# A fused attention and two-layer MoE kernel: the first half of its operations in another order, and copies and subtractions on other engines

## The chip, the cores and the metric

The kernel runs on one core of a Trainium2 chip. A core has five engines that run side by side, each with its own instruction queue that it works off strictly in order: TensorE (PE, matrix multiplication), VectorE (DVE), ScalarE (ACT), GpSimd (POOL) and SyncE (SP, which here issues every DMA). They wait for each other by semaphores. The metric is the device time of one execution in microseconds; smaller is better.

## The reference, cut to what matters

```python
# attention: batch 4, heads 8, sequence S = 576, head size 64
scores = (q @ k.T) / sqrt(64)
cum    = cumsum(log(clip(f, 1e-4, 1)))                # a forget gate: 32 rows of 576
attn   = softmax(causal_mask(scores + cum[:, None] - cum[None, :]))
x      = (attn @ v) as (2304 tokens, 512)
# first layer, d_ff = 2048; w is delivered as float64
h = x @ w_in;  g = max(h, 0) + alpha * min(h, 0);  x = g @ w_out
# second layer, the same sizes
h = x @ w_in2; g = h * tanh(log1p(exp(h)));        out = g @ w_out2
```

## The kernel before

Nothing in this kernel is issued where it is written. The functions `stage_T`, `stage_M`, `stage_S`, `stage_R`, `stage_V`, `group_a` and `moe_block` only record operations in a `Plan`: 5,138 of them, each with a number, an engine, what it reads and writes, and a function that issues its instructions. At the end `emit` walks through one list of operation numbers and issues them. Since each engine works off its queue in order, this list sets the order on all five engines.

**Attention** runs over 16 pairs of heads. For each pair:
- `stage_T` copies q and k into the tiles `QM` and `KM` (ACT, L478). Three more rows of `KM` come by DMA (SP, L736) from the running sums of the forget gate; the running sums are made once, at the start, by a chain of DVE and ACT operations on the tile `Pt` (L689 to L695).
- `stage_M` finds each row's maximum: twelve matmuls (PE, L773) and after each a reduction on DVE (L780), which writes `nmx` or a column of `M`. They share three PSUM banks. Five transposes (PE, L792) and two copies turn `M` into the tile `BQ`.
- `stage_S` forms the scores in four pieces (PE, L817), ACT takes the exponential into `Pt` (L827), POOL masks the diagonal blocks (L835).
- `stage_R` adds five parts of `Pt` with four additions into `accp` (L853, of 896, 128, 640 and 384 columns; all on POOL before), and PE sums over partitions (L865).
- `stage_V` multiplies by v in two windows (PE, L899), and DVE writes the result to `X` (L905).

In pair 0 each matmul of `stage_M` and each piece of `stage_S` is followed by a dummy matmul (L676), and thirty such dummies, which need only the tile `ident` made by POOL, stand ahead of everything on PE.

The matmuls use PE's array in three shapes: 128 rows by 128 columns (L773, L792, and all of the MoE), 64 rows by 128 (L817), and 128 rows by 64 (L865, L899).

**The MoE** runs over six blocks of 384 tokens. Float64 weights come in by DMA and are put together as float32 by ACT and DVE (`wb`, L556 to L562), then split into a high and a low part, the low part by a subtraction (L488); activations are split in the same way (`xh`, `xl`, `g`). A product is three matmuls (L943 to L945, L1008 to L1010, L1019 to L1021). `group_a` computes the first four slices of the first layer for a block; for three blocks its matmuls are meant to fill gaps of the attention, between its matmuls on PE.

For a copy or a subtraction that can run on two or three engines, `add` picks its home. Before, this goes by the place of the operation in its stage: `ENG.get(key, ...)`, with 39 entries, so each repetition of a stage has the same home. The order before is a written list of the first 3,391 operations; the rest follow as the planner `schedule`, a list scheduler with priorities (`PRIO`) and assumed costs, puts them.

Of the kernel before, what the change touches and what calls it, by code (L numbers as in the profile page):

```python
# [174 lines left out]


class Plan:

    HOP = {"PE": 0.25, "ACT": 0.2, "DVE": 0.22, "POOL": 0.15, "SP": 1.0, "SWAP": 0.0}
    OWN = {"PE": 0.0, "ACT": 0.14, "DVE": 0.12, "POOL": 0.1, "SP": 1.0, "SWAP": 0.0}  # L190
# [1008 lines left out]
```

## Time and profile before

| what | value |
|---|---|
| median of 3 runs | 1011.56 us (1011.18 to 1013.09) |
| the profiled execution's own time | 1013.04 us |
| its span on the core | 1011.3 us |
| PE busy | 999.3 us (99%) |
| DVE, ACT, POOL busy | 740.1, 536.1, 341.8 us |

The profiled execution is one run at the upper edge of the three. The span is what its trace shows, from the first instruction to the last; 1.7 us of its time lie outside. A PE that is "busy" isn't a PE at full speed: matmuls are pipelined, and a matmul that waits inside the pipeline counts as busy.

### The profile page before, as it was taken

The page shows a single profiled execution, that of the slowest core. Times are in us where ns is not written, and L with a number is a line of the kernel's source. Part 1 is how long each engine was busy: PE and PEld are TensorE (multiplying, and loading weights), DVE is VectorE, ACT ScalarE, POOL GpSimd, SP SyncE. Part 2 cuts the span into 40 slices and gives each one's busy share as a digit, 9 for nine tenths or more (in the row PEclk, how much of TensorE's full clock was granted, in tenths as well). Part 3 has the DMA queues.
Part 4 walks back from the last instruction along what each step waited for, and adds up shares of the span by engine and source line. Part 5 has one row for each costly group of instructions (what it writes and reads, how often), then busy time and mean ns, then how long its engine had stood idle before and what let it go on. Part 6 is the DMA issues. An engine that isn't in the chain of part 4 may idle for free.

```text
span 1011.3 us, 16560 instructions
## 1 busy us (share of the span) xinstructions
PE 999.3 (99%) x5900; PEld 899.6 (89%) x5900; DVE 740.1 (73%) x1751; ACT 536.1 (53%) x1127; POOL 341.8 (34%) x351
## 2 busy tenths in 40 slices
PE   7999999999999999999999999999999999999998
PEld 6667777777999999999999999999998899989997
DVE  7787666555687765655666679877788888977975
ACT  5777676654555543233334466555454544555553
POOL 4676545545355421010101012342323322423321
PEclk9999999999999999999999999999999999999999
DMA  5344122120224323334443353000000000000000
GB/s 159 104 116 125 50 75 71 38 60 14 82 86 146 125 94 125 126 103 142 131 154 101 112 155 117 1 1 32 1 31 2 0 32 1 11 21 1 32 1 31
DMA packets 55394, 71.02 MB, mean 70 GB/s; under 512 B 6672, under 2 KB 32272, under 8 KB 55312
## 3 DMA queue, kind: packets, MB, share of 16 engines
q1 hardware_dynamic: 55312, 69.97, 21.9%
q8 instruction: 46, 0.75, 0.3%
q14 instruction: 36, 0.29, 0.1%
HBM read 56.60 MB, written 13.33 MB: 69 GB/s over the span
## 4 chain that ended last, share of the span: by engine, by line
PE 96%; DVE 3%; ACT 1%; issue 1%; DMA 0%; DVEq 0%; ACTq 0%
PE b L943 13%; PE b L945 13%; PE b L944 13%; PE b L1008 7%; PE b L1021 7%; PE b L1020 7%; PE b L1019 7%; PE b L1010 7%; PE b L1009 6%; PE b L817 6%; PE b L899 4%; PE b L773 3%; PE b L865 2%; PE b L792 1%; DVE junk L780 1%; DVE wb L558 1%
## 5 line engine op out<-in xcount | busy, mean ns | idle before, releaser
L943 PE MATMUL b<-xh,w 128*128 128x384 f32 x768 | 258.7, 337 | 0.2 <-DVE x L480 0.2
L945 PE MATMUL b<-xl,w 128*128 128x384 f32 x768 | 257.4, 335 | 0.0
L944 PE MATMUL b<-xh,w 128*128 128x384 f32 x768 | 257.2, 335 | 0.0
L1000 POOL TENSOR_TENSOR x<-x 128x384 f32<-128x384 f32 x96 | 112.3, 1171 | 250.3 <-DVE x L998 187.0
L943 PEld LDWEIGHTS b<-xh,w 128*128 128x128 f32 x768 | 144.2, 188 | 5.3 <-issue 1.0
L944 PEld LDWEIGHTS b<-xh,w 128*128 128x128 f32 x768 | 144.2, 188 | 3.1
L945 PEld LDWEIGHTS b<-xl,w 128*128 128x128 f32 x768 | 144.2, 188 | 0.0
L1008 PE MATMUL b<-g,w 128*128 128x384 f32 x384 | 130.1, 339 | 0.8 <-DVE x L971 0.7
L1010 PE MATMUL b<-g,w 128*128 128x384 f32 x384 | 128.4, 334 | 0.0
L1009 PE MATMUL b<-g,w 128*128 128x384 f32 x384 | 128.4, 334 | 0.0
L478 ACT CAST g<-x 128x384 fp32r<-128x384 f32 x120 | 61.4, 513 | 113.3 <-POOL x L1000 56.3
L1021 PE MATMUL b<-w,g 128*128 128x512 f32 x288 | 113.2, 393 | 0.0
L1020 PE MATMUL b<-w,g 128*128 128x512 f32 x288 | 113.0, 392 | 0.0
L1019 PE MATMUL b<-w,g 128*128 128x512 f32 x288 | 112.8, 392 | 0.0
L780 DVE CUSTOM_DVE_ANT_0 junk<-b,tri 128x320 f32<-128x320 f32 (+3 forms) x160 | 69.4, 434 | 45.9 <-PE b L773 36.1
L488 DVE TENSOR_TENSOR g<-x,g 128x384 fp32r<-128x384 f32 x102 | 73.3, 722 | 37.3 <-ACT g L478 36.7
L556 ACT ACTIVATE wb<-raw 128x256 f32<-128x256 f32 x128 | 52.9, 432 | 56.8 <-DMA raw<-in_moe_w_out_dram 27.6
L488 POOL TENSOR_TENSOR xl<-X,xh 128x384 fp32r<-128x384 f32 x18 | 20.8, 1161 | 168.6 <-ACT xh L478 165.8
L827 ACT ACTIVATE Pt<-b 128x288 f32<-128x288 f32 (+1 forms) x128 | 58.1, 502 | 33.4 <-PE b L817 31.4
L1008 PEld LDWEIGHTS b<-g,w 128*128 128x128 f32 x384 | 72.1, 188 | 3.6 <-DVE x L971 1.5
L558 DVE TENSOR_SCALAR wb<-wb 128x256 int32<-128x256 int32 x128 | 43.6, 356 | 42.6 <-ACT wb L556 42.2
L992 ACT ACTIVATE x<-x,two 128x384 f32<-128x384 f32 x96 | 58.6, 613 | 28.6 <-DVE x L990 28.3
(93 smaller groups left out, 1911.1 us busy)
## 6 DMA issues: line engine op xcount, KB each, us to landing
raw<-in_moe_w_in_dram SPq DMA_DIRECT2D x64, 256.0 KB
raw<-in_moe_w_out_dram SPq DMA_DIRECT2D x64, 256.0 KB
wd<-wb SPq DMA_DIRECT2D x32, 256.0 KB
raw<-wd SPq DMA_DIRECT2D x32, 256.0 KB
kt<-in_k_dram SPq DMA_DIRECT2D x16, 288.0 KB
qt<-in_q_dram SPq DMA_DIRECT2D x16, 288.0 KB
out_dram<-x SPq DMA_DIRECT2D x18, 256.0 KB
vt<-in_v_dram SPq DMA_DIRECT2D x16, 256.0 KB
```

The costliest lines, as they stand in the source:

```text
L488: plan.add(engs, 0.0, at, lambda e: (nc.gpsimd if e == "POOL" else nc.vector).tensor_tensor(out=out(), in0=in0(), in1=in1(), op=ALU.subtra ...
L780: nc.vector.tensor_tensor_reduce(out=junk[ql, :z - a], in0=ps()[ql, :z - a], in1=tri[ql, x0 + a:x0 + z], scale=-1.0, scalar=BIG if n == 0 ...
L943: nc.tensor.matmul(ps[:, :NB], w[:, 0, c], xh[c], start=(c == 0), stop=False)
L944: nc.tensor.matmul(ps[:, :NB], w[:, 1, c], xh[c], start=False, stop=False)
L945: nc.tensor.matmul(ps[:, :NB], w[:, 0, c], xl[c], start=False, stop=(c == KC - 1))
L1000: add("POOL", c_pool(NB, 2.2), lambda e, m: nc.gpsimd.tensor_tensor(out=m, in0=e, in1=m, op=ALU.mult), [ek, mk], [mk])
L1008: nc.tensor.matmul(ps[:, :NB], w[:, 0, c], g[:, 0], start=first, stop=False)
L1009: nc.tensor.matmul(ps[:, :NB], w[:, 1, c], g[:, 0], start=False, stop=False)
L1010: nc.tensor.matmul(ps[:, :NB], w[:, 0, c], g[:, 1], start=False, stop=last)
L1019: nc.tensor.matmul(ps, g[:, 0, sl], w[:, 0], start=first, stop=False)
L1020: nc.tensor.matmul(ps, g[:, 0, sl], w[:, 1], start=False, stop=False)
L1021: nc.tensor.matmul(ps, g[:, 1, sl], w[:, 0], start=False, stop=last)
```

## The change

The planner, `PRIO` and `ENG` go. All 5,138 operations stand in one written list, and the home of each copy and subtraction is looked up by the operation's own number, so that two repetitions of a stage can have different homes. The list differs from the order before in its first 2,600 places; the last 2,538 are the same. The same 5,138 operations are done, with the same numbers.

```diff
-PRIO = {'': {0: -17.5, 1: -17.2, ...
-ENG = {('A0g', 0): 'ACT', ('A0g', 2): 'ACT', ('A0g', 3): 'POOL', ...
 ORDER = [int(x) for x in """
-11 29 12 23 15 22 16 17 28 25 14 27 32 5 36 21 35 34 3 31 24 13 33 38 26 89 56 84 9 10 55 113 90 85 18 20 86
...
 """.split()]
+HOME = {}
+HOME.update(dict.fromkeys((int(x) for x in """
...
+""".split()), "ACT"))
...
     def add(self, eng, cost, at, fn, ...):
         n = len(self.ops)
-        key = tuple(self.key)
         self.key[1] += 1
-        at += PRIO.get(key[0], {}).get(key[1], 0.0)
         if isinstance(eng, dict):
-            alt, e = eng, ENG.get(key, next(iter(eng)))
-            eng, cost, f = e, alt[e], fn
+            e = HOME.get(n, next(iter(eng)))
+            eng, cost, f = e, eng[e], fn
             fn = lambda f=f: f(e)
...
-    def schedule(self, nexts, left, eng, cost, prio, lag, dma, uses=()):
...
     def emit(self):
+        done = [False] * len(self.ops)
+        left = [len(ns) for _, ns in self.uses]
...
+        spare = {g: list(range(len(x))) for g, x in self.groups.items()}
+        for n in ORDER:
+            assert all(done[d] for d in self.ops[n][4])
+            for u in mine[n]:
+                if ("use", u) not in self.taken:
+                    self.taken["use", u] = spare[self.uses[u][0]].pop(0)
+            self.ops[n][3]()
...
-        head = set(ORDER)
-        order = ORDER + [n for n in order if n not in head]
-        for n in order:
-            ops[n][3]()
```

Homes that change, counted over the whole program: 59 operations go from POOL to DVE (23 additions of `stage_R`, 21 subtractions of weights, 15 of activations), 34 from ACT to DVE (copies), 29 from DVE to POOL (subtractions of activations), 13 from DVE to ACT.

In the rows below, line numbers are those of each file: L780, L558, L560, L562 of before are L739, L517, L519, L521 of the changed file, L773 is L732, L865 is L824, L792 is L751, L899 is L858. `ISA` is the reduction and the short read of its result that follows it.

First DVE, from the running sum of the forget gate (L691 and L650) into the reductions of pair 0. Before:

```order
L691 SCALAR_TENSOR_TENSOR Pt_123<-Pt_123,tri 32x576
L697 MEMSET bvec 128x1
L697 MEMSET bvec 3x1 x2
L558 TENSOR_SCALAR wb_92<-wb_92 128x256 x2
L695 SCALAR_TENSOR_TENSOR Pt_123<-Pt_123 32x576
```

and, five rows and the first three reductions further on:

```order
L780 ISA M_142 128x1
L558 TENSOR_SCALAR wb_92<-wb_92 128x256
L780 ISA junk,M_142<-b_69,tri,nmx 128x256
L780 ISA M_142 128x1
L560 SCALAR_TENSOR_TENSOR wb_92<-raw_91,wb_92 128x256
L780 ISA junk,M_142<-b_70,tri 64x64
L780 ISA M_142 64x1
L562 SCALAR_TENSOR_TENSOR wb_92<-raw_91,wb_92 128x256
```

The changed kernel, from the same running sum on:

```order
L650 SCALAR_TENSOR_TENSOR Pt_123<-Pt_123,tri 32x576
L656 MEMSET bvec 128x1
L656 MEMSET bvec 3x1 x2
L654 SCALAR_TENSOR_TENSOR Pt_123<-Pt_123 32x576
L664 MEMSET KM_0_136 64x576
L517 TENSOR_SCALAR wb_92<-wb_92 128x256 x2
```

and from the end of its third reduction on:

```order
L739 ISA M_142 128x1
L739 ISA junk,M_142<-b_69,tri,nmx 128x256
L739 ISA M_142 128x1
L739 ISA junk,M_142<-b_70,tri 64x64
L739 ISA M_142 64x1
L739 ISA junk,M_142<-b_71,tri 64x64
L739 ISA M_142 64x1
```

The last operation of the gate's chain (L695, L654) now stands ahead of the weight operations, and between the reductions of pair 0 the weight operations stand later: six of them lie between the third and the tenth reduction before, one now. On the other engines at this place: on POOL `ident` is made first now, where five fills stood ahead of it; on SP the k of pair 0 is the second load, where it was the sixth, and the q of pair 2 and one load of `BK` stand ahead of the first weights of `w_out`; on ACT the two weight activations (L556) stand behind the first copy of k instead of ahead of it.

Then PE, where `stage_R` and `stage_V` of pair 0 stand between matmuls of pairs 1 and 2. Before:

```order
L773 MATMUL b_70<-KM_0_134,QM_0_130 128x192
L865 MATMUL b_65<-Pt_122,ones 64x128 x2
L865 MATMUL b_65<-accp,ones 64x160 x2
L865 MATMUL b_66<-accp,ones 64x288 x2
L773 MATMUL b_71<-KM_1_135,QM_1_131 128x192
L899 MATMUL b_69<-Pt_122,vt_145 64x256 x2
L899 MATMUL b_69<-Pt_122,vt_145 64x128 x2
L792 MATMUL b_67<-ident,M_142 128x128 x3
L792 MATMUL b_68<-ident,M_142 128x128 x2
L899 MATMUL b_70<-Pt_122,vt_145 64x320 x6
L899 MATMUL b_70<-Pt_122,vt_145 64x192 x2
L899 MATMUL b_70<-Pt_122,vt_145 64x64 x2
```

The changed kernel:

```order
L824 MATMUL b_68<-accp,ones 64x288 x2
L732 MATMUL b_69<-KM_0_136,QM_0_132 128x256
L732 MATMUL b_71<-KM_1_137,QM_1_133 128x320
L751 MATMUL b_65<-ident,M_142 128x128 x3
L751 MATMUL b_66<-ident,M_142 128x128 x2
L858 MATMUL b_70<-Pt_122,vt_145 64x320 x6
L858 MATMUL b_70<-Pt_122,vt_145 64x192 x2
L858 MATMUL b_70<-Pt_122,vt_145 64x64 x2
L858 MATMUL b_71<-Pt_122,vt_145 64x256 x2
L858 MATMUL b_71<-Pt_122,vt_145 64x128 x2
L776 MATMUL b_65<-qt_126,kt_129 128x448
```

The two windows of `stage_V`, which stood apart with matmuls of full shape ahead of and between them, follow each other now, and the next scores follow straight on them. Over the whole program the shape of the array changes from one matmul to the next 150 times before and 117 times now.

## Rows read from the trace of the kernel before

**Rows 1.** The page, part 1: busy us, share of the span, instructions.

```profile
PE 999.3 (99%) x5900; PEld 899.6 (89%) x5900; DVE 740.1 (73%) x1751; ACT 536.1 (53%) x1127; POOL 341.8 (34%) x351
```

**Rows 2.** Busy time by stretch: stretch, length, PE, PEld, DVE, ACT, POOL, clock, DMA.

```profile
0.00:25.00 25.00, 19.48 (x116) 16.50 (x116) 19.45 (x63) 13.47 (x25) 11.89 (x27) 0.91 0.51 161
...
450.00:500.00 50.00, 50.00 (x291) 50.00 (x290) 31.52 (x78) 17.93 (x43) 3.32 (x3) 1.00 0.42 132
...
sum 400.00, PE 397.21 PEld 337.75 DVE 276.77 ACT 236.43 POOL 186.08; mean PE 56.74 PEld 48.25 DVE 39.54 ACT 33.78 POOL 26.58
```

**Rows 3.** PE's longest wait: us in total, times, longest.

```profile
PE b L676 <- POOL ident masks.py:199: 3.8, 1, 3.8
```

**Rows 4.** Timelines of the first 21 us: start, length, engine, operation [idle before].

```profile
3.79 8.41 PE L676 MATMUL b<-ident 128*128 128x128 f32 x60 [3.79 <-POOL ident masks.py:199]
...
7.11 0.68 ACT L694 ACTIVATE Pt<-Pt 32x576 fp32r<-32x576 f32 x1 [0.41 <-DVE bvec L697]
...
7.33 1.65 DVE L558 TENSOR_SCALAR wb<-wb 128x256 int32<-128x256 int32 x2
8.89 0.74 DVE L695 SCALAR_TENSOR_TENSOR Pt<-Pt 32x576 fp32r<-32x576 f32 x1
...
9.71 1.57 SPq L736 DMA_DIRECT2D KM<-Pt  x2
...
12.39 0.49 DVE L780 CUSTOM_DVE_ANT_0 junk<-b,tri 128x320 f32<-128x320 f32 x1 [0.58 <-PE b L773]
...
13.72 0.48 DVE L780 CUSTOM_DVE_ANT_0 junk<-b,tri,nmx 128x256 f32<-128x256 f32 x1 [0.17 <-PE b L773]
...
14.70 0.29 DVE L558 TENSOR_SCALAR wb<-wb 128x256 int32<-128x256 int32 x1 [0.48 <-ACT wb L556]
14.90 0.48 DVE L780 CUSTOM_DVE_ANT_0 junk<-b,tri,nmx 128x256 f32<-128x256 f32 x1
...
20.66 0.36 DVE L780 CUSTOM_DVE_ANT_0 junk<-b,tri 128x192 f32<-128x192 f32 x1 [0.56 <-PE b L773]
```

**Rows 5.** The stretch of the slow clock, columns as in Rows 2.

```profile
20.50:27.30 6.80, 6.48 (x29) 4.38 (x27) 4.71 (x18) 3.58 (x8) 1.23 (x2) 0.50 0.25 85
```

**Rows 6.** The chain that ended last, 98 to 136 us: start, us, what.

```profile
99.81 0.80 PE b L899 x8
100.61 0.98 PE b L865 x12
101.59 2.05 PE b L899 x20
...
121.36 1.13 PE b L865 x12
...
128.85 2.21 PE b L899 x20
...
132.03 0.65 PE b L899 x8
```

**Rows 7.** Durations by shape and home: count, busy us, mean ns, idle before.

```profile
L853 POOL TENSOR_TENSOR accp<-Pt 128x896 f32<-128x896 f32 x16 | 33.7, 2106 | 3.2 <-PE b L865 1.8 <-ACT Pt L827 0.6 <-POOL Pt L835 0.6
...
L488 DVE TENSOR_TENSOR g<-X,g 128x384 fp32r<-128x384 f32 x72 | 41.2, 586 | 19.1 <-ACT g L478 18.9
...
L488 DVE TENSOR_TENSOR w<-raw,w 128x512 fp32r<-128x512 f32 x32 | 22.2, 713 | 7.1 <-ACT w L478 7.0
```

**Rows 8.** DVE from 20 to 140 us: busy time, and its longest wait.

```profile
20.00:140.00 120.00, 118.22 (x888) 86.05 (x888) 90.62 (x319) 88.21 (x182) 70.34 (x84) 0.97 0.32 94
...
DVE junk L780 <- PE b L773: 13.7, 18, 2.0
```

**Rows 9.** DVE and POOL from 33 to 37 us, and L558 over the whole run (min/median/max).

```profile
33.66 2.06 DVE L558 TENSOR_SCALAR wb<-wb 128x256 int32<-128x256 int32 x2
...
33.97 2.94 POOL L853 TENSOR_TENSOR accp<-accp,Pt 128x640 f32<-128x640 f32 x2
...
L558 DVE TENSOR_SCALAR wb<-wb x128: 277/285/1629, 7.3 to 568.1; 128x256 int32<-128x256 int32 x128
```

More of the change, by code (lines that the diff above doesn't have):

```diff
@@ L1 @@
 from contextlib import ExitStack
-from heapq import heappop, heappush
 import concourse.bass as bass
@@ L21 @@
-ENG = {('A0g', 0): 'ACT', ('A0g', 2): 'ACT', ('A0g', 3): 'POOL', ('A1g', 0): 'ACT', ('A2g', 2): 'ACT', ('A2g', 3): 'DVE', ('A3g', 0): 'DVE', ('AX', 1): 'DVE', ('AX', 2): 'ACT', ('AX', 3): 'DVE', ('AX', 4): 'ACT', ('AX', 5): 'DVE', ('AX', 7): 'DVE', ('B0', 4): 'DVE', ('B3', 4): 'DVE', ('H0', 4): 'ACT', ('H0', 7): 'DVE', ('H1', 13): 'ACT', ('H1', 14): 'DVE', ('NM2', 1): 'ACT', ('NM2', 2): 'ACT', ('O1', 3): 'DVE', ('O1', 5): 'ACT', ('R2', 3): 'POOL', ('T2', 2): 'ACT', ('T2', 3): 'ACT', ('WF', 2): 'DVE', ('X0', 0): 'ACT', ('X0', 1): 'POOL', ('X0', 2): 'ACT', ('X0', 3): 'POOL', ('X0', 4): 'ACT', ('X0', 6): 'ACT', ('X0', 7): 'POOL', ('X1', 0): 'ACT', ('X1', 3): 'POOL', ('X1', 5): 'POOL', ('X1', 6): 'ACT', ('X1', 7): 'POOL'}
@@ L25 @@
 ORDER = [int(x) for x in """
[150 rows of a table removed]
-""".split()]
-class Plan:
-    HOP = {"PE": 0.25, "ACT": 0.2, "DVE": 0.22, "POOL": 0.15, "SP": 1.0, "SWAP": 0.0}
-    OWN = {"PE": 0.0, "ACT": 0.14, "DVE": 0.12, "POOL": 0.1, "SP": 1.0, "SWAP": 0.0}
-    DMA_LAG = 0.65
-    PASSES = 10
-    SWITCH = 0.2
-    STAY = 1.5
[224 rows of a table added]
+""".split()]
+HOME = {}
+HOME.update(dict.fromkeys((int(x) for x in """
[4 rows of a table added]
+""".split()), "ACT"))
+HOME.update(dict.fromkeys((int(x) for x in """
[14 rows of a table added]
+""".split()), "DVE"))
+HOME.update(dict.fromkeys((int(x) for x in """
@@ L196, in __init__ @@
+2242 2244 2394 2396 2550 2552 2556 2706 2708 2712 3329 3331 3333 3616 3618 3620 3918 3920 3922 4220
+4222 4224 4522 4524 4526 4824 4826 4828
+""".split()), "POOL"))
+class Plan:
     def __init__(self):
@@ new lines, in emit @@
+    def emit(self):
+        done = [False] * len(self.ops)
+        left = [len(ns) for _, ns in self.uses]
+        mine = [[] for _ in self.ops]
+        for u, (_, ns) in enumerate(self.uses):
+            for n in ns:
+                mine[n].append(u)
+        spare = {g: list(range(len(x))) for g, x in self.groups.items()}
[5 more added lines that the diff above has]
+            self.ops[n][3]()
+            done[n] = True
+            for u in mine[n]:
@@ L320, in schedule @@
                 left[u] -= 1
                 if not left[u]:
-                    heappush(wait[eng[u]], (ready[u], prio[u], u))
-        return order, start, found
-    def emit(self):
-        ops = self.ops
-        N = range(len(ops))
-        eng = [o[0] for o in ops]
-        dma = [o[5] if o[0] == "SP" else 0.0 for o in ops]
-        def graph(found):
-            deps = [dict.fromkeys(o[4], True) for o in ops]
-            for u, (_, before) in found.items():
-                if before is not None:
-                    deps[self.uses[u][1][0]].update(dict.fromkeys(self.uses[before][1], True))
-            users = [[] for _ in ops]
-            for n in N:
-                for d in deps[n]:
-                    users[d].append(n)
-            return [list(d) for d in deps], users
-        def pace(slow):
-            cost = [o[1] * (1.0 if o[0] == "PE" else 1.0 + 0.1 * (slow - 1.0)) for o in ops]
-            return cost, {e: x * (slow if e != "SP" else (1.0 + slow) / 2) for e, x in self.HOP.items()}
-        def total(order, users, slow):
-            cost, hop = pace(slow)
-            ready, free, queue = [0.0] * len(ops), dict.fromkeys(eng, 0.0), 0.0
-            now, door = "", 0.0
-            for n in order:
-                e = eng[n]
-                start[n] = max(free[e], ready[n], door if ops[n][7] else 0.0)
-                end = start[n] + cost[n]
-                if ops[n][7]:
-                    door = end
-                if e == "PE":
-                    end += self.SWITCH if ops[n][6] != now else 0.0
-                    now = ops[n][6]
-                free[e] = end
-                if dma[n]:
-                    end = queue = max(queue, end + self.DMA_LAG) + dma[n]
-                for u in users[n]:
-                    ready[u] = max(ready[u], end + (hop[e] if eng[u] != e else self.OWN[e]))
-            return max(free.values())
-        cost, hop = pace(1.2)
-        start = [0.0] * len(ops)
-        prio = [o[2] for o in ops]
-        best = None
-        deps0, users0 = graph({})
-        for _ in range(self.PASSES):
-            order, at, found = self.schedule(
-                users0, [len(d) for d in deps0], eng, cost, prio,
-                lambda a, b: hop[eng[a]] if eng[b] != eng[a] else self.OWN[eng[a]], dma, self.uses)
-            deps, users = graph(found)
-            t = sum(total(order, users, x) for x in (1.0, 1.2, 1.6))
-            if best is None or t < best[0]:
-                best = (t, order, found, users)
-            _, back, _ = self.schedule(
-                deps, [len(u) for u in users], eng, cost, [-at[n] - cost[n] for n in N],
-                lambda a, b: (hop[eng[b]] if eng[a] != eng[b] else self.OWN[eng[b]]) + dma[b] + self.DMA_LAG * (dma[b] > 0), None)
-            prio = [-back[n] - cost[n] for n in N]
-        _, order, found, users = best
-        head = set(ORDER)
-        order = ORDER + [n for n in order if n not in head]
-        self.taken = {("use", u): b for u, (b, _) in found.items()}
-        for n in order:
-            ops[n][3]()
-        self.start = start
-        self.total = total(order, users, 1.0)
@@ L394, in fox_attention__then__moe_prelu__then__moe_mish @@
+                    spare[self.uses[u][0]].append(self.taken["use", u])
+        assert all(done)
 @with_exitstack
```

65 lines of the change are left out of this document (removed), and 391 rows, old and new, of tables (HOME, ORDER).

## The prediction

> **What bounds the kernel now.** I read the page first: PE is busy for 999.3 us, 99% of the span [rows 1]. So only PE's own time counts, and the first question is where PE isn't dense. The table of busy time by stretch says it [rows 2]: 5.5 us of idle PE in the first 25 us, 2.8 us in the 400 us behind that (400 less 397.2), and none from 450 to 500 us, inside the MoE. The changed half of the order covers the attention and a part of the first MoE layer. In the MoE part PE has nothing to win; whatever the change brings must come from the attention, roughly the first 300 us, and whatever it brings there shifts everything behind it, since a full PE follows.
>
> The list of waits names one long one, 3.8 us for `ident` at the very start [rows 3]. That is little of the loss that a gapless PE could win. The larger part of PE's loss stands in no list of waits, because a matmul that is held up inside the pipeline counts as busy. Two things of that kind are visible: a price for each change of the array's shape, and a stretch of half clock early on. Both come below.
>
> **The change part by part.**
>
> *The start.* The timelines of the first 21 us [rows 4] show the chain on which the first reductions hang: ACT's scaling of the running sum (L694) ends at 7.79 us; DVE's last operation of the gate (L695) could begin there plus a hop, at about 8.0, but stands behind two weight operations and begins at 8.89; SP issues the rows of `KM` at 9.71, as soon as it ends; the first reduction begins at 12.39. In the new order L695 comes first: 0.9 us earlier. Between reductions, DVE then sits 0.48 us waiting for an ACT weight operation at 14.70, with the fourth reduction queued behind it: that one starts at 14.90, 1.18 us after the third (13.72), where the first three came 0.67 apart (12.39 to 13.72). The new order has no weight work there, which gives back 0.5 us, and five more weight operations leave the stretch, of which I count 0.2 us, since they fitted mostly beside the reductions' waits. Sum: 1.6 us by the twelfth reduction (20.66), on which transposes and first scores hang. Bounds: 0.7, if the copies of q and k on ACT hold up the start (two weight operations now stand among them), and 2.9, if all five others count at 0.29 us like the one at 14.70. The earlier `ident` lets the thirty dummies begin earlier, by up to the 3.79 us that they wait now. It is worth nothing: they take 8.4 us and then end before the rows of `KM` can land, and PE has a hole of up to 2.9 us (3.8 less 0.9) ahead of the first maximum. On SP the loads for pairs 0 and 2 move ahead of the first weights of `w_out`; only `group_a` needs those, later on PE: nothing.
>
> *Half clock.* From 20.5 to 27.3 us the granted clock is 0.50, the lower level, 1.2 GHz, with PE busy 6.48 of 6.80 us [rows 5]. From 450 to 500 us it is 1.00, 2.4 GHz [rows 2]. What PE did before it fell: the dummies until 12 us, and then matmuls paced by the reductions, one in some 0.7 us. The new order keeps this shape, a little denser. So I leave the stretch as it is: 0. Bounds: one half of 6.8 us, 3.4 us, won if it goes, or lost if the new hole brings another one.
>
> *Changes of shape.* The chain of work shows the price of one [rows 6]. The same eight, twelve and twenty matmuls appear with and without one: L899 x8 takes 0.80 us behind matmuls of full shape and 0.65 inside a run of its own shape; L865 x12 1.13 and 0.98; L899 x20 2.21 and 2.05. That is 0.15 us per change. The new order has 117 instead of 150, 33 fewer, nearly all behind pair 1: 33 x 0.15 is 5.0 us. Some of them stood where PE waited for an operand anyway; I take 0.13 each, 4.2 us. Bounds: 3.3 (0.10 each) and 5.3 (0.16).
>
> *PE's other waits.* The 2.8 us of visible idle behind 25 us [rows 2] are waits for reductions, exponentials and copies. A new order can take them away or make others. I take half as won, 1.4 us; bounds 0 and 2.8.
>
> *Other homes.* Ten of the 23 additions that move from POOL to DVE belong to pairs 0 to 7. The trace has no such addition on DVE. Its POOL price for 896 columns is 2106 ns; the nearest rows on DVE are subtractions of two SBUF operands, 586 ns for 384 columns and 713 for 512 [rows 7], about 1 ns a column, so 896 columns are 1.09 us, 640 are 0.84, 384 are 0.59, 128 are 0.33. Three, one, four and two of these are 7.1 us more on DVE; four subtractions of activations go the other way there, 2.3 us less. Net 4.8 us more in a stretch where DVE is busy 90.6 of 120 us and itself waits 13.7 us for the very matmuls PE is late with [rows 8]. So most of it lies beside DVE's waits: I count a quarter, 1.2 us of loss. Bounds 0 and 4.8. Behind 300 us the moves add work to DVE, with PE at full and DVE busy 31.5 of 50 us [rows 2]: nothing, as long as no product comes late.
>
> *Sum.* 1.6 + 4.2 + 1.4 - 1.2 = 6.0 us. Against the profiled execution's 1013.04 us that is 1007.0; this run was 1.5 us above the median, so against the median of 1011.56 it is 1005.6 us.
>
> **A rule that bears on the homes.** In the trace, two DVE operations (L558) take 2.06 us together at 33.66, while POOL works on two additions; over the whole run this operation has a median of 285 ns and a maximum of 1629 [rows 9]. So DVE and POOL seem to hold each other up. The Trainium skill says in "SBUF — State Buffer", "Who interferes with whom", that a DVE instruction with two SBUF inputs contends with a GpSimd instruction that reads SBUF. By that rule each addition moved to DVE could wait for whatever POOL is doing. It speaks against the move, and makes a rival below.
>
> **The rivals.**
>
> *A larger gain*, 1000 us: the half clock goes, or the waits hidden inside "busy" go as well. For it: PE's early matmuls come denser, without weight work between the reductions. Worked out: 6.0 + 3.4 for the clock and 1.4 for the other half of the visible waits is 10.8, 1000.8 us. Against it: the reductions still pace PE until about 20 us, and PE gets a hole at 10 us.
>
> *No change*, 1011 us: a merged run of one shape has to wait for the last of its operands, so that each change saved becomes a wait of the same size. For it: both windows of `stage_V` now follow each other and need `uu` of the same pair. Then 4.2 us turn to nothing, and so do the 1.4 of the waits; 1.6 - 1.2 are left, 1011.2. Against it: between them PE has work of other pairs and of `group_a` in the order.
>
> *DVE and POOL hold each other up*, on the other side. The place is the attention, where 23 additions and eight subtractions move to DVE while POOL still runs masks and the other additions. The price by the trace: L558's largest excess was 1.3 us (1629 less 285 ns); I take 0.5, between nothing and that, and 31 x 0.5 is some 16 us of DVE time. It decides against the gain when more than 7.2 of these 16 us come to lie on PE's path, since 6.0 + 1.2 are won otherwise. With 10 of them, 1011.56 - 7.2 + 10 is 1014.4 us. Against it: each of these operations leaves POOL, so there is less to meet; POOL was busy 70.3 of 120 us [rows 8].
>
> *Another stretch of half clock* costs 3.4 us and still ends at 1009.0; it is inside the forecast's own range.
>
> **How the numbers follow.** A measurement of this kernel can't tell differences under about 0.2%, 2.0 us, from none. Chances: the forecast, from 1001.5 to 1009.5 us, 0.56; the larger gain 0.20; no change 0.13; DVE and POOL 0.11. Faster is the first two, 0.76; same 0.13; slower 0.11. The predicted time is 1005.6 us. The range reaches from the larger gain, 1000.0, to 1011.6: it leaves out the slower case and the third of the larger gain that may lie below 1000, 0.18 in all.
>
> **What would show it.** Right: the first reduction at about 11.5 us and the twelfth near 19; L865 x12 mostly at 0.98; no weight operation of more than 0.5 us ahead of a reduction; PE as dense as before behind 300 us, and the whole MoE shifted by some 6 us. Wrong: additions L853 on DVE well above 1.1 us for 896 columns, PE waiting for them (behind `accp`) or for `X`; a second stretch at clock 0.50; waits of PE in the first MoE layer, on `w` or `g`, where there were none.

## The result and the profile after

| what | before | changed |
|---|---|---|
| median | 1011.82 us, 7 runs (1011.18 to 1017.25) | 1020.44 us, 7 runs (1019.39 to 1023.66) |
| ratio to before, 95% interval | | 1.0087 [1.0064, 1.0110] |
| profiled execution, its span | 1013.04, 1011.3 us | 1020.44, 1018.7 us |

The change makes the kernel slower, by 8.8 us going by the ratio (8.6 by the medians). The forecast was 1005.6 us and faster; the time lies outside its range, on the other side. The first part of the changed kernel's page answers to [rows 1]: PE has the same number of instructions and is busy for the same time, in a longer span, so what was added is waiting.

```profile
PE 998.4 (98%) x5900; PEld 902.2 (89%) x5900; DVE 778.8 (76%) x1802; ACT 525.2 (52%) x1106; POOL 294.0 (29%) x321
```

**Where the time goes.** The table of busy time by stretch of the changed kernel answers to [rows 2] (stretch, length, PE, PEld, DVE, ACT, POOL, clock, DMA share, GB/s):

```profile
0.00:25.00 25.00, 19.67 (x112) 17.28 (x113) 18.28 (x57) 13.13 (x23) 10.21 (x27) 0.91 0.47 150
...
50.00:75.00 25.00, 23.23 (x186) 15.92 (x185) 20.97 (x72) 17.42 (x37) 16.31 (x21) 1.00 0.34 93
...
300.00:350.00 50.00, 48.85 (x278) 47.60 (x277) 45.85 (x106) 26.88 (x63) 10.80 (x8) 1.00 0.34 111
350.00:400.00 50.00, 49.50 (x284) 48.98 (x283) 36.49 (x84) 17.26 (x39) 7.61 (x7) 1.00 0.36 116
400.00:450.00 50.00, 46.84 (x268) 45.88 (x267) 30.85 (x66) 12.39 (x30) 8.14 (x7) 1.00 0.32 97
450.00:500.00 50.00, 48.55 (x277) 47.56 (x276) 31.62 (x77) 16.40 (x41) 3.30 (x3) 1.00 0.41 129
```

From 300 to 500 us, where PE had been dense, it is now idle for 6.3 us. Waits inside the pipeline come on top. To see them I asked of both traces when PE had done equal amounts of its work (each matmul group counted with its undisturbed time). The changed kernel against the profiled execution of before, in us; the places are an estimate, since other choices of the undisturbed time move them by tens of us of work, while the loss from the lowest point on stays at 9.7 to 9.9 us:

```
PE work done      20    50   120   180   220   260   300   340   380   400   440   460 to the end
changed - before +1.2  +2.3  +0.4  -0.8  -2.4  -2.5  -0.7  +0.8  +2.3  +4.8  +7.0  +7.4
```

So the start loses, the attention behind 50 us gains some 4 to 5, and between 260 and 460 us of work, the first MoE layer, 9.9 us are lost; nothing happens behind it. The list of PE's waits from 310 to 500 us (total, times, longest) names what [rows 2] had none of:

```profile
PE b L902 <- DVE X L927: 2.7, 4, 1.3
PE b L902 <- DVE X L930: 2.5, 2, 2.3
PE b L968 <- DVE w L447: 0.5, 1, 0.5
```

L927 and L930 (before: L968, L971) are, in `prelu`, the activation of the first layer, the DVE operations that read a slice's PSUM bank last: L927 where the first operation of `prelu` was on ACT (L921), L930 where it was on DVE (L923). The first matmul L902 (before: L943) of a slice waits for one of them because only it frees the bank that the slice four further on uses. How much room there is can be read from both traces, from 310 to 500 us: from the end of that operation to the L902 that takes the bank, before, a median of 3.8 us over 47 slices, and under 0.5 us once; after, 1.5 us over 44, and under 0.5 us twelve times.

The chain of work of the changed kernel around its longest wait (start, us, what) shows who is late:

```profile
422.36 0.42 DVE wb L521
422.78 0.48 DVE g L447
423.26 0.14 SPq L550
...
423.91 4.67 DMA raw<-in_moe_w_in_dram
...
428.69 0.43 ACT wb L515
429.12 0.39 ACT X L921
...
429.53 0.04 DVE X L927
...
430.06 0.61 DVE X L923
...
431.06 0.56 DVE X L930
...
431.66 0.44 PE b L902
```

Read it upwards. The L902 at 431.66 waits for L930, which with its L923 finishes the slice that held the bank; the product of that slice was there at 426.8 us. Both stand in DVE's queue behind L927 of another slice, and that waits for its L921 on ACT. The product of this L921 was there at 422.1 us, and the part of `X` that it writes was free when POOL had read it, at 425.7:

```profile
424.70 1.01 POOL L447 TENSOR_TENSOR g<-X,g 128x384 fp32r<-128x384 f32 x1 [3.67 <-ACT g L437]
```

But ahead of it in ACT's queue stands L515, a conversion of a weight for the second layer (not needed before 570 us) whose load lands at 428.6. The load was issued late, since DVE freed its buffer late. So an operation that could have run waits 3.3 us behind one that can't, and a second queue waits behind it.

**The start.** The timeline of the first 21 us answers to [rows 4]:

```profile
3.82 1.43 DVE L648 TENSOR_SCALAR Pt<-Pt 32x576 f32<-32x576 f32 x1
...
6.71 1.34 DVE L650 TENSOR_TENSOR_SCAN Pt<-Pt,tri 32x576 f32<-32x576 f32 x1
...
8.80 0.75 DVE L654 SCALAR_TENSOR_TENSOR Pt<-Pt 32x576 fp32r<-32x576 f32 x1 [0.52 <-ACT Pt L653]
...
12.30 0.48 DVE L739 CUSTOM_DVE_ANT_0 junk<-b,tri 128x320 f32<-128x320 f32 x1
...
12.44 0.41 SPq L683 DMA_DIRECT2D qt<-in_q_dram  x1
...
16.58 1.36 ACT L437 CAST QM<-qt 64x576 fp32r<-64x576 f32 x2 [3.30 <-DMA qt<-in_q_dram]
...
17.20 0.49 DVE L739 CUSTOM_DVE_ANT_0 junk<-b,tri 128x320 f32<-128x320 f32 x1
...
19.28 0.29 DVE L517 TENSOR_SCALAR wb<-wb 128x256 int32<-128x256 int32 x1 [1.58 <-ACT wb L515]
19.48 0.48 DVE L739 CUSTOM_DVE_ANT_0 junk<-b,tri 128x320 f32<-128x320 f32 x1
...
20.74 0.35 DVE L739 CUSTOM_DVE_ANT_0 junk<-b,tri 128x192 f32<-128x192 f32 x1
...
20.90 0.61 PE L732 MATMUL b<-KM,QM 128*128 128x320 f32 x1 [2.54 <-DVE wb L519]
```

L654 is 0.1 us earlier, not 0.9; the twelfth reduction comes at 20.74, before at 20.66. The ninth reduction, at 17.20, is early, but the tenth stands behind a conversion, which waits for ACT, which waits for a load of q: the same pattern as at 428 us. The stretch of lower clock of [rows 5] has become longer, 10.0 us instead of 6.8:

```profile
20.50:27.30 6.80, 6.40 (x24) 5.06 (x26) 4.69 (x21) 4.88 (x10) 1.67 (x2) 0.50 0.40 121
27.30:30.50 3.20, 3.20 (x16) 2.22 (x14) 1.29 (x6) 0.88 (x2) 0.00 (x0) 0.50 0.00 0
```

### The profile page after: what moved, and what is told of

Read it like the earlier page. It is cut to its first block, busy times and chain, and to the rows that moved or that the text cites. A ratio compares the mean times of both kernels' runs of the same rounds, so it can differ in the third digit from the quotient of the medians.

```text
span 1018.7 us, 16555 instructions
## 1 busy us (share of the span) xinstructions
PE 998.4 (98%) x5900; PEld 902.2 (89%) x5900; DVE 778.8 (76%) x1802; ACT 525.2 (52%) x1106; POOL 294.0 (29%) x321
## 4 chain that ended last, share of the span: by engine, by line
PE 80%; DVE 9%; DMA 5%; issue 2%; ACT 2%; SPq 1%; DVEq 0%; ACTq 0%
PE b L902 11%; PE b L904 11%; PE b L903 11%; PE b L980 7%; PE b L979 7%; PE b L978 7%; PE b L776 5%; PE b L967 4%; PE b L968 4%; PE b L969 4%; PE b L858 4%; PE b L732 3%; DMA raw<-in_moe_w_out_dram 2%; DVE wb L521 2%; DVE wb L519 2%
## 5 line engine op out<-in xcount | busy, mean ns | idle before, releaser
L902 PE MATMUL b<-xh,w 128*128 128x384 f32 x768 | 259.2, 338 | 5.3 <-DVE X L927 2.7
L902 PEld LDWEIGHTS b<-xh,w 128*128 128x128 f32 x768 | 144.2, 188 | 12.0 <-DVE X L927 4.7
L968 PE MATMUL b<-g,w 128*128 128x384 f32 x384 | 128.6, 335 | 0.5 <-DVE w L447 0.5
L739 DVE CUSTOM_DVE_ANT_0 junk<-b,tri 128x320 f32<-128x320 f32 (+3 forms) x160 | 69.4, 434 | 34.0 <-PE b L732 25.4
L515 ACT ACTIVATE wb<-raw 128x256 f32<-128x256 f32 x128 | 52.5, 431 | 81.3 <-DMA raw<-in_moe_w_out_dram 29.5
L517 DVE TENSOR_SCALAR wb<-wb 128x256 int32<-128x256 int32 x128 | 41.9, 336 | 51.9 <-ACT wb L515 51.2
L786 ACT ACTIVATE Pt<-b 128x288 f32<-128x288 f32 (+1 forms) x128 | 57.7, 503 | 36.7 <-PE b L776 30.5
L969 PEld LDWEIGHTS b<-g,w 128*128 128x128 f32 x384 | 72.1, 188 | 2.3 <-DVE g L447 2.3
L967 PEld LDWEIGHTS b<-g,w 128*128 128x128 f32 x384 | 72.1, 188 | 1.5 <-issue 1.1
```

What stands on the lines that cost most here:

```text
L739: nc.vector.tensor_tensor_reduce(out=junk[ql, :z - a], in0=ps()[ql, :z - a], in1=tri[ql, x0 + a:x0 + z], scale=-1.0, scalar=BIG if n == 0 ...
L902: nc.tensor.matmul(ps[:, :NB], w[:, 0, c], xh[c], start=(c == 0), stop=False)
L967: nc.tensor.matmul(ps[:, :NB], w[:, 0, c], g[:, 0], start=first, stop=False)
L968: nc.tensor.matmul(ps[:, :NB], w[:, 1, c], g[:, 0], start=False, stop=False)
L969: nc.tensor.matmul(ps[:, :NB], w[:, 0, c], g[:, 1], start=False, stop=last)
```

## The experiments

Each kernel carries a written list and homes of its own; "hybrid" is the new attention with the old first layer. Ratios are to the kernel before, run on the same chip in the same batch.

**Which part, and order or homes.** Two kernels take the change apart by kind, two by place (the cut is the last matmul group L858 of the attention, at some 255 us).

```diff
 # e1_order: new ORDER, old HOME        # e2_homes: old ORDER, new HOME
 # e3_att:
-ORDER = new
+head = new[:new.index(last_L858) + 1]
+ORDER = head + [n for n in old if n not in head]
+HOME = new homes for head, old homes behind
 # e4_moe: the same with old and new exchanged
```

> The new order with the old homes. Theory 'order': in the first MoE layer the new order puts weight conversions that wait for their DMA ahead of the activation operations on ACT and DVE, so PE waits for its PSUM banks there whatever the homes are; then the loss stays and the time is 1018 to 1022 us. Theory 'homes': DVE, busy 90 of 100 us from 250 to 350 us because of the operations moved to it, is late by itself; then the loss of some 10 us goes and the time is 1008 to 1012 us. Theory 'pair': the order was fitted to its homes, and each alone is worse than both together: over 1023 us.

Measured: 1051.16 us, 1.0382 [1.0365, 1.0400].

> The old order with the new homes. Theory 'order': about the time of before, 1010 to 1014 us. Theory 'homes': DVE gets the added work in the old order as well, and the time is 1018 to 1022 us. Theory 'pair': slower than the changed kernel, over 1023 us, since subtractions now run on engines whose queues were ordered for other work.

Measured: 1033.30 us, 1.0224 [1.0203, 1.0245].

> New order and homes up to the last attention matmul of L858 (some 255 us), behind it the old order and the old homes. Both theories put the loss behind this point: the time is that of before less the 2.5 us that the attention gained in the trace, 1008 to 1010 us, and PE is dense from 260 us on. If the loss is a debt of the attention (weights or slices left over that the first MoE layer has to make up for), it stays: 1014 to 1020 us.

Measured: 1010.43 us, 0.9985 [0.9975, 0.9995]. The time lies just above the range expected; PE is dense from 300 us on.

> Old order and homes up to the last attention matmul of L858, new ones behind it. Both theories: before's time plus the loss of the first MoE layer, some 10 us: 1020 to 1024 us. If the loss is a debt of the new attention: 1010 to 1014 us.

Measured: 1023.80 us, 1.0114 [1.0098, 1.0130].

The places are clear: the attention gains 1.5 us and the first layer loses 11.5 behind the old attention, 10.3 behind the new one (1.0087 against 0.9985). The kinds are not: order and homes hold only together, as the third theory said. A fifth kernel asked the same of the first layer alone:

```diff
-HOME = new homes
+HOME = new homes up to the last L858, old homes behind; ORDER = new
```

> The changed kernel with the old homes behind the last attention matmul of L858 only; order unchanged. Theory 'waiting conversions': the loss stays, 1018 to 1022 us. Theory 'DVE too full': the loss goes, 1009 to 1012 us. Theory 'pair' (the order holds only with the durations it was made with; POOL takes 1.2 us where DVE takes 0.6): slower than the changed kernel, over 1023 us, most of it here, since the whole order with old homes lost 13 us of PE time between 250 and 350 us.

Measured: 1035.37 us, 1.0217 [1.0201, 1.0233]. "DVE too full" was expected to gain here and lost 13 us (1.0217 against 1.0087). This says that POOL's and ACT's longer times don't fit the new order, not that DVE is innocent.

**Operations behind waiting conversions.** In the changed kernel's list only the places of second-layer conversions against other operations of ACT and DVE were changed, for example around 428 us on ACT:

```diff
 L437 CAST g<-X 128x384
-L515 ACTIVATE wb<-raw 128x256
 L921 ACTIVATE X<-b 128x384
+L515 ACTIVATE wb<-raw 128x256
 L515 ACTIVATE wb<-raw 128x256
```

> The changed kernel, with one thing moved: from 380 to 505 us, activation operations that by its trace were ready earlier go ahead of the conversions of second-layer weights on ACT and DVE that stood before them and waited for their load; 22 operations on ACT go ahead so, the order on PE is the same. Theory 'waiting conversions' (the loss comes from operations queued on ACT and DVE behind conversions whose load hasn't landed): the waits of PE at 405, 418, 429, 484 and 490 us go (0.5, 0.7, 2.4, 0.4 and 1.6 us, 5.6 in all), 1013 to 1016 us. Theory 'DVE too full' (the loss comes from the operations that moved to DVE): no change, 1018 to 1022 us.

Measured: 1016.84 us, 1.0042 [1.0023, 1.0061], a gain as 'waiting conversions' says, but short of its range.

> The kernel with activation operations put ahead of waiting conversions, once more: in its own trace one wait of 1.9 us for a DVE operation behind conversions is left at 486 us, with a stretch of lower clock behind it; 25 more operations on ACT and DVE go ahead of conversions of second-layer weights between 350 and 505 us. Theory 'waiting conversions': that wait and the low clock behind it go, and the slow half of its runs with them: 1012 to 1015 us. Rival: moving them only moves the wait on, 1016 to 1019 us.

Measured: 1014.14 us, 1.0027 [1.0014, 1.0039]. The wait at 486 us is gone, as expected; runs of up to 1017.7 us are not. The busy time of this second kernel, against the last two rows of the changed one above:

```profile
400.00:450.00 50.00, 50.00 (x289) 49.74 (x288) 31.98 (x72) 15.49 (x37) 7.95 (x7) 1.00 0.32 100
450.00:500.00 50.00, 50.00 (x291) 49.95 (x290) 33.69 (x85) 16.48 (x42) 4.34 (x4) 1.00 0.41 127
```

The 4.6 us of idle PE from 400 to 500 us are gone with DVE as busy as before, and with the same homes. Of the 8.8 us, 6.1 came back (1.0087 against 1.0027; by the two intervals together, between 3.5 and 8.7) by order on ACT and DVE alone: the queues of PE, POOL and SP are those of the changed kernel. That is the main cause, shown.

Two kernels put all weight work behind the cut, loads and stores too, at the other kernel's places, counted in matmul groups of PE:

```diff
-weight work (load_w, store_w) at the new places      # f2: at the old places
+weight work at the old places, in the new order      # f2: at the new places, in the old order
```

> The changed kernel with the weight work behind the last L858 (loads, conversions, splits, stores) at the places, and with the homes, that it had before, counted in matmul groups of PE; everything else as changed. Theory 'waiting conversions': the conversions come where their loads have landed, 1010 to 1014 us. Theory 'DVE too full': the other moved operations stay, 1017 to 1021 us. If the old places only fit the old order of the activations, more waits appear: over 1022 us.

Measured: 1074.86 us, 1.0610 [1.0590, 1.0629].

> The kernel before with only the weight work behind the last L858 at its new places and homes. Theory 'waiting conversions': the loss appears here, 1017 to 1022 us. Theory 'DVE too full': a third of the added DVE work comes along (19 subtractions of 0.7 us), 1011 to 1014 us.

Measured: 1088.08 us, 1.0737 [1.0720, 1.0755]. The first falls under its third case (over 1022 us), the second is far outside of both theories; the places fit only the list that they come from. They tell nothing between the theories.

**What is left in the first layer.** The second kernel still loses some 4 us of PE between 260 and 370 us.

```diff
-L515, L517, L519, L521, L437, L447 of first-layer weights, 255 to 380 us, ahead of activations that are ready earlier
+the same behind them
```

> The kernel with activation operations ahead of waiting conversions of second-layer weights, and now also ahead of the weight work of the first layer from 255 to 380 us (67 operations on ACT and DVE go ahead). In its parent's trace PE still loses some 4 us there: 1.25 at 267, 0.7 at 311, 1.1 at 328, 0.3 at 348, 0.6 at 370. Theory 'waiting conversions': they go, 1009.5 to 1012 us. Rival 'DVE too full' (there the work itself is late: operations of DVE take two to three times as long beside POOL's subtractions, and DVE is 90% busy): the weights come late in place of the activations, 1013 to 1018 us.

Measured: 1025.52 us, 1.0125 [1.0102, 1.0149], slower than either theory said. Now the weights come late; PE's waits from 255 to 380 us begin with

```profile
PE b L902 <- ACT x L437: 1.7, 2, 1.2
PE b L967 <- ACT w L437: 1.6, 1, 1.6
```

Here both kinds of work are needed at once, and putting all of one ahead cost more than it gave. So this cure does not reach the rest; whether a choice between single operations would, no run shows. Taking work off DVE there:

```diff
-HOME: seven first operations of the activation on DVE, two subtractions of X on DVE (299 to 370 us)
+HOME: seven on ACT, two on POOL
```

> The kernel with activation operations ahead of waiting conversions of second-layer weights, with nine of DVE's added operations between 299 and 370 us back at their old homes: seven first operations of the activation to ACT, two subtractions to POOL; same order. 5.4 us less on DVE, where it is 90% busy. If the loss that is left (4 us between 260 and 370 us) comes from a DVE that is too full there: 1 to 2 us faster than its parent, 1011.5 to 1013 us. Theory 'pair' (any home other than the one the order was made with makes something late): slower, 1015 to 1020 us.

Measured: 1014.27 us, 1.0018 [1.0001, 1.0036]. It can't be told from its parent, and lies between the two expectations. The two subtractions on POOL add to what DVE meets there: PE's waits for the subtraction of `g` from 255 to 380 us are 3.0 us, 1.8 in the parent. So this run doesn't rule out a DVE that is too full, which in the parent is busy for 4.00 of 4 us from 264 to 268 us and for 3.93 from 326 to 330, where PE loses. A place in the parent's timeline shows one thing that a schedule of fixed durations can't know:

```profile
327.48 1.29 POOL L447 TENSOR_TENSOR w<-wb,w 128x512 fp32r<-128x512 f32 x1 [4.98 <-ACT w L437]
327.99 1.19 DVE L447 TENSOR_TENSOR g<-X,g 128x384 fp32r<-128x384 f32 x1
...
329.24 0.44 PE L969 MATMUL b<-g,w 128*128 128x384 f32 x1 [0.81 <-DVE g L447]
```

The subtraction of `g` takes 1.19 us beside POOL where its median is 0.55, and PE waits for it. How much of the 4 us comes from this was not tried by itself.

**The start.** From the hybrid, first the conversions between the ninth and the twelfth reduction were moved, then one load as well.

```diff
 # h1_front, DVE
-L517 TENSOR_SCALAR wb_92<-wb_92 128x256
 L739 ISA junk,M_142<-b_71,tri 128x320
...
 L739 ISA M_142 128x1
-L519 SCALAR_TENSOR_TENSOR wb_92<-raw_91,wb_92 128x256
+L517 TENSOR_SCALAR wb_92<-wb_92 128x256 x2
+L519 SCALAR_TENSOR_TENSOR wb_92<-raw_91,wb_92 128x256 x2
 # t1_load, SP
 L683 DMA kt_128<-in_k_dram 128x576
+L683 DMA qt_125<-in_q_dram 128x576
 L695 DMA KM_0_134<-Pt_123 3x1x576
...
-L683 DMA qt_125<-in_q_dram 128x576
```

> The hybrid of new attention and old first layer, with four DVE operations moved: the second weight's conversions (L517, L519, both halves), which in the trace of the changed kernel stand between the ninth and the twelfth reduction of pair 0, go behind the twelfth. Theory 'waiting conversions' (one mechanism at the start and in the first layer): the tenth reduction no longer waits behind a conversion that waits for ACT, which waits for a load of q; the twelfth reduction comes at about 19.2 instead of 20.7 us, and the time falls by 1.0 to 2.0 us from the hybrid's, to 1008.5 to 1009.5. Rival: the twelfth isn't what PE waits for, or the pair behind it takes the gain back: within 0.5 us of the hybrid, 1010 to 1011.

Measured: 1010.06 us, 0.9982 [0.9973, 0.9991], against the hybrid's 0.9985: no difference that can be told. The timeline has the twelfth reduction at 18.79 us, two us earlier, as expected, and PE starts on pair 1 no earlier:

```profile
16.30 1.37 ACT L437 CAST QM<-qt 64x576 fp32r<-64x576 f32 x2 [2.99 <-DMA qt<-in_q_dram]
...
21.03 0.87 PE L732 MATMUL b<-KM,QM 128*128 128x320 f32 x2 [2.67 <-ACT KM L437]
```

The wait that the list gave to L519 was one for the copies of pair 1, that is for its load of q, issued at 12.45 us behind the rows of `KM`, which wait for the gate until 9.65.

> The hybrid with the four conversions behind the twelfth reduction, and one load more moved on SP: q of pair 1 goes ahead of the rows of KM (where the old order has it), instead of three places behind them. In the parent's trace PE waits 2.7 us at 21 us, at the end of a chain that begins with this load: issued at 12.4 us instead of 3.7, landing at 16.3, its copies, then the rows of KM for pair 1. Theory 'late load': the copies come at about 13 us, the wait goes, and with it, in part of the runs, the stretch of lower clock: 1007 to 1008.5 us. Rival: the transfer takes the place of another that is needed as much: 1009.5 to 1011 us.

Measured: 1007.89 us, 0.9952 [0.9935, 0.9969], the fastest kernel of this study, 4.9 us faster than before. Its timeline, and its busy time in the stretch of [rows 5]:

```profile
3.69 0.43 SPq L683 DMA_DIRECT2D qt<-in_q_dram  x1
...
13.33 1.37 ACT L437 CAST QM<-qt 64x576 fp32r<-64x576 f32 x2
...
19.94 0.53 PE L732 MATMUL b<-KM,QM 128*128 128x320 f32 x2 [1.57 <-DVE wb L519]
```

```profile
20.50:27.30 6.80, 6.46 (x46) 4.55 (x46) 5.97 (x26) 5.20 (x11) 1.76 (x3) 1.00 0.33 96
```

The load is issued 8.8 us earlier, the copies come 3 us earlier, PE starts 1.1 us earlier, and in this execution the clock stays at its upper level. Of the 11 runs without the load moved none had a mean granted clock over 0.998; of the 7 with it, five had 0.999 or 1.000.

> The changed list and all its homes, with three places mended: q of pair 1 loaded ahead of the rows of KM, four conversions behind the twelfth reduction, activations ahead of waiting conversions of second-layer weights (the run of 1014.1 us). If the start costs what theory 'late load' says: 1.5 to 3 us less than that run, 1011 to 1012.5 us. If the start's loss is taken up behind it: 1013.5 to 1014.5 us.

Measured: 1012.56 us, 0.9998 [0.9984, 1.0011]. With its three places mended the whole change is as fast as before. Against t1_load, which has the old first layer, 4.7 us are still lost.

**The attention's gain.** Two hybrids keep the old order for its first 288 or 614 places (`+head = old[:288]`, `old[:614]`), and one takes the kernel before and only joins runs of a shape (ten matmul groups moved, as in the change: `ST1` of pair 0 behind `ST2`, `V2` behind `R2`; 128 changes of shape instead of 148, counted by groups without the dummies of pair 0; by the trace's matmuls, 132 instead of 150).

> The hybrid of new attention and old first layer, with the first 288 places of the old order (some 60 us) kept ahead of the new attention. By the times of equal PE work in the two traces the hybrid is 0.6 to 1.4 us behind the old kernel from 40 to 80 us of work and gains only behind that: 1008.5 to 1010 us if the front's loss goes, 1010 to 1013 if the joint costs as much.

Measured: 1010.06 us, 0.9977 [0.9968, 0.9987], on the border of the two expectations.

> Old order for the first 614 places (pairs 0 to 6, some 115 us), the new attention behind it, and the old first layer. If the attention's gain lies behind 120 us (joined runs of one shape, 2.9 us between 140 and 220 us in the times of equal work): 1008 to 1009.5 us. If it hangs on the new front: 1011 to 1013 us.

Measured: 1008.90 us, 0.9969 [0.9957, 0.9981]. The gain lies behind 120 us, where the new order has 52 changes of shape instead of 76: 3.1 us for 24, or 0.13 us each, as the prediction took it, if all of it is theirs; the homes differ there too, and no run parts the two.

> The kernel before with ten matmul groups on PE moved up or down by a few places, so that runs of one array shape join: 128 changes of shape instead of 148; nothing else. If a change costs 0.13 to 0.15 us of PE time: 2.6 to 3.0 us faster than before, 1008.5 to 1009.5 us. If a joined run only waits for its last operand: no difference, 1011 to 1013 us.

Measured: 1018.32 us, 1.0068 [1.0054, 1.0081]. Joining by itself loses: PE is busy only 21.87 us from 25 to 50 us, where it was busy 24.04 before. Eight of the ten moves are in pairs 0 to 4, where PE waits for reductions and exponentials anyway. That fits a price which is won only where the operands are there; no run tests this by itself.

## Why the prediction was wrong, point by point

- **The step that failed** is the end of "Other homes": behind 300 us the moves cost "nothing, as long as no product comes late". Products came late, and the sum had no term for that: the first layer loses 11.5 us. I read from [rows 2] that PE was full and DVE busy 31.5 of 50 us, and took the free time for room. That row is from 450 to 500 us; from 250 to 350, DVE was busy 75.3 of 100 us before and is busy 90.2 now. And what PE waits for is one operation in a queue, and its place there is set by the order, which I had looked at only in the attention. Conversions that wait for loads stand ahead of activations before as well. ACT's waits for their loads and buffers from 280 to 480 us (total, times, longest), before:

```profile
ACT wb L556 <- DMA raw<-in_moe_w_out_dram: 17.0, 8, 5.3
ACT wb L556 <- DMA wd<-wb: 7.9, 4, 4.5
ACT wb L556 <- DMA raw<-in_moe_w_in_dram: 4.8, 9, 1.9
```

  and in the changed kernel:

```profile
ACT wb L515 <- DMA wd<-wb: 19.4, 5, 8.6
ACT wb L515 <- DMA raw<-in_moe_w_out_dram: 15.7, 5, 5.7
ACT wb L515 <- DMA raw<-in_moe_w_in_dram: 12.4, 6, 4.1
```

  That is 29.7 and 47.5 us. What covered them before, as I read it, was the 3.8 us between a bank's release and its next use; the new order had 1.5 left. In h2_ready2, with these conversions behind the activations, the waits are 30.5 us and the room is 2.5. Shown for 6.1 of the 8.8 us; the other 4 to 5 us that the new first layer loses are located, from 260 to 370 us, their cause is open.
- **The start, 1.6 us**: nothing came. "The new order has no weight work there" was true for the first nine reductions and false for the last three. The move of loads on SP, counted as nothing, was the larger miss: I looked at what the loads of pairs 0 and 2 passed, and not at the load of pair 1 that went behind a waiting issue. At the gate, L648 took 1.43 us where the same operation had taken 0.45, which ate the 0.9 us (behind it, ahead of the scan, stand two memsets in both kernels). Before:

```profile
3.82 0.45 DVE L689 TENSOR_SCALAR Pt<-Pt 32x576 f32<-32x576 f32 x1
```

- **Half clock, 0**: wrong, inside its bound of 3.4. The stretch is 3.2 us longer. Moreover not every run of before has it: of 29 in one batch, 21 had a mean granted clock of 0.999 or more. The profiled execution had 0.996. In the changed kernel all seven runs had 0.996 or less.
- **Changes of shape, 4.2 us** (33 times 0.13 is 4.3): the price fits, 0.13 us, if the gain behind 120 us is all theirs. The row that was to show it, L865 x12 at 0.98, does not: it stays at 1.13 since it now leads its run. The other 28 matmuls of the run (x8 and x20 in [rows 6]) show it:

```profile
122.20 1.13 PE b L824 x12
...
154.40 2.71 PE b L858 x28
```

  2.71 is 0.65 and 2.05 of [rows 6], without a price. Ten of the changes saved lie ahead of 120 us; a gain by them is not seen, since the front as a whole loses (0.9985 with it, 0.9969 with the old one).
- **PE's other waits, 1.4 us won**: the table of busy time has 4.0 us of idle PE from 25 to 250 us, where before had 2.1. Lost, not won.
- **Other homes in the attention, 1.2 us lost**: the prices were right (estimated 1.09 us for 896 columns):

```profile
L812 DVE TENSOR_TENSOR accp<-Pt x6: 1078/1085/1140, 36.1 to 244.7; 128x896 f32<-128x896 f32 x6
```

  PE's list of waits in the changed kernel has none for `accp`: a cost on this path is not seen.
- **The rival** "DVE and POOL hold each other up" had the right sign and the wrong place. Added over all DVE instructions that overlap an operation of POOL, what they take beyond the median of their line and shape is 68 us before and 71 after, 46 and 47 of it behind 500 us. In the attention, from 25 to 255 us, where the rival put some 16 us more, it is 6.5 us before and 8.7 after. What changed is that in the first layer it now falls on a queue with less room: from 255 to 380 us DVE is busy 110.8 of 125 us, before 96.3. What that costs is not shown.
- The mark "waits of PE in the first MoE layer, on `w` or `g`, where there were none" came true, mostly as waits for `X`; the stretch at clock 0.50 did not become a second one but grew. Of the marks for being right, the first reduction came at 12.30 us and not 11.5, the twelfth at 20.74 and not 19, and PE was not dense behind 300 us.

## What to carry to other kernels

In an in-order queue ask of each operation what it waits for, and who stands behind it: an operation that waits for a load should have nothing behind it that could run and is needed soon. A full bottleneck engine says nothing about how nearly its operands are late; measure the time from release to next use before you move anything. An order and the homes it was made for go together, and an order made from fixed durations has to leave room for the ones that vary: loads (6.1 us here, in the first layer), and DVE beside POOL.

## What was not expected of the hardware

- **One DVE operation, two durations.** L517, a `TENSOR_SCALAR` on 256 columns, takes 0.29 us in the mean over the 116 that meet no operation of POOL and 0.78 over the 12 that do; its extremes in the changed kernel:

```profile
L517 DVE TENSOR_SCALAR wb<-wb x128: 280/290/1978, 10.3 to 576.3; 128x256 int32<-128x256 int32 x128
```

  L648 took 1.43 us beside POOL's memsets, but 0.45 before, with memsets of POOL beside it as well; so this row leaves its cause open. The prediction named only two-input operations. The Trainium skill says in "SBUF — State Buffer", "Who interferes with whom", that `tensor_scalar` too can take the port pair that DVE shares with GpSimd, when its operands meet certain conditions, and that the other then waits for the whole instruction; the trace agrees in that such an operation is held up (up to 1.98 us), and doesn't show which port it was.
- **How busy PE was does not tell whether the clock falls.** In h1_front PE was busy 2.15 of the 4.5 us from 16 to 20.5, and from 20.5 to 24 us the granted clock was 0.55, nearly all of it at the lower of its two levels (1.2 GHz). In t1_load, which differs in one load, issued 8.8 us earlier, PE was busy 2.72 of the 4.5 us, and the clock stayed at 1.00 (2.4 GHz). But before, PE was busy 3.75 of the 4.5 us and the clock fell to 0.50, while r2_late, with the same 3.75, stayed at 1.00; and t2_mended, with the load moved, was busy 2.65 and had 0.50 from 20.5 to 24 us. So neither the load nor this gap settles it, and what does is open.
